# A second table of places for an attention, Fourier and feed-forward kernel

## The chip, the cores and the metric

The kernel runs on one core of a Trainium2 chip. A core has five engines that run side by side, each with its own instruction stream, worked through strictly in order: TensorE (PE) multiplies matrices, VectorE (DVE) and ScalarE (ACT) do elementwise work, GpSimd (POOL) does elementwise work and issues some transfers, and SyncE (SP) issues most transfers. The engines wait for each other on semaphores. The metric is the device time of one execution, in microseconds (us); lower is better. The kernel before took 1082.76 us, the median of 3 runs (1081.66 to 1085.46).

## The reference

There are 8 batches, each with 8 heads, 576 positions and 64 channels per head. The attention part adds two results: a full softmax attention over queries, keys and values that are averaged in groups of four positions, repeated back to full length, and a softmax attention in which a position sees only neighbours less than 4 away. The heads are laid side by side to x with 512 channels, and then:

```python
X = np.fft.fft(np.fft.fft(x, axis=1), axis=2)
u = x + np.real(X)
un = (u - mean(u)) / np.sqrt(var(u) + 1e-6)
out = u + np.maximum(un @ w_ch1, 0.0) @ w_ch2     # 512 -> 2048 -> 512
```

## The kernel before, in words

**Stages.** Of each batch, five overlapping stretches of the sequence are five units (class Unit). A unit's queries and keys come in by one transfer (`Unit.load`, line 707), its values by another (`Unit.load_v`, line 711). PE makes the local scores (line 740), DVE the maxima (752), ACT the exponentials (759), PE transposes them (772) and multiplies by the values (800), and DVE scales the result (820) into one of two tiles, xa or xb, that all batches share. Beside it class Pooled does the averaged attention of a whole batch: `sum_in` (DVE, 723) adds up queries and keys of every unit in groups of four, `pool_v` (PE, 567) does it for the values of all five units, and `scores` (593), `values` (642) and `result` (660) work on the sums in three groups.

**Fourier stage.** Class Mix folds the batch (`cross`, `channels`, `fold`), multiplies along the sequence on PE (`sequence`, 909), then along the channels (`mix`, 945 and 949), and DVE unfolds the result (968). Three kinds of rows go out to memory on SP's queue: xa and xb as they are (`store_local`, 1001 and 1002, to tensors ux), the mixed rows (`store_mixed`, 982, to tensors um) and the last rows of a pair of batches (`store_ends`, 988). xa and xb can be written for the next batch only when `store_local` has read them.

**Feed-forward.** The 36 tiles of 128 rows are taken in blocks of four. Blocks 0 to 2 (class Block) load the parts, sum them, normalise, transpose (`turn`, 1162) and multiply: `first` is twelve matmuls (1189), `high` and `low` (ACT 1193, DVE 1197) split the hidden row in two parts, `second` is twelve matmuls (1209 to 1211), `finish` (1214) adds the input. Products of two split numbers take three matmuls. The other blocks run in pairs (class Super) by a scheme with seven products in place of eight (`product`, 1348), which needs sums of the inputs (`add_up` on POOL, 1315, `sum_high` on ACT, 1326, `sum_low` on DVE, 1330) and differences of the weights. Class Differences makes those, one after another for eight pairs of weight tiles: `rejoin` (DVE, 1069) adds two parts of a weight tile into the tiles raws[0] and raws[1], `differ` (POOL, 1079) subtracts quarters of them from each other, `high` (ACT, 1083) and `low` (POOL, 1087) split the differences, and `keep` (SP, 1092) stores them.

**Chains that matter below.** The tiles raws are few. The next `rejoin` overwrites what `differ` reads, and the next `differ` overwrites what `keep` stores. The same raws serve later as scratch: raws[0] holds a transposed tile that `sum_high` and `sum_low` read, and it then takes `save` (ACT, 1368), which copies the first product out of its bank so that PE may go on adding to that bank. All PE results go to eight banks; a step that needs a bank waits until the one that used it is done.

**The order.** Every step is put into a list by the function `at`. For each kind of step the table TURNS holds a list of numbers, its places, one for each instance in the order in which the program's plans name them; the list of steps is sorted by place, and in that order each engine gets its instructions. The places run from 0 to 1954, up to the first steps of the paired blocks. Later steps have due times that a plan computes, and come after all places. No scheduler changes the order, so an instruction that waits holds up all behind it on its engine.

```python
    def at(fn, *args, t=0.0):
        ...
        place = next(places.get(name, iter(())), None)
        events.append((place is None, t if place is None else place, len(events), partial(fn, *args)))
    ...
    with tc.manual_schedule():
        for *_, fn in sorted(events, key=lambda e: e[:3]):
            fn()
```

Of the kernel before, what the change touches and what calls it, by code (L numbers as in the profile page):

```python
# [27 lines left out]
        49, 124, 252, 388, 530, 652, 781, 917,  # L28
    ),
    "Pooled.copy_v": (  # L30
        51, 131, 256, 395, 535, 659, 789, 918,
    ),
    "Pooled.scores": (
        38, 30, 33, 138, 95, 104, 270, 210, 229, 394, 347, 367, 539, 489, 505, 672, 604, 605, 786, 749, 759,
        937, 864, 890,
    ),
    "Pooled.maxima": (
        54, 32, 36, 149, 98, 110, 275, 212, 234, 402, 356, 382, 545, 495, 511, 675, 608, 614, 796, 751, 761,
        945, 873, 895,
    ),  # L40
    "Pooled.exps": (
        64, 37, 44, 154, 107, 125, 280, 215, 242, 418, 372, 393, 552, 504, 531, 688, 613, 629, 797, 757, 773,
        950, 878, 914,
    ),
    "Pooled.transpose_p": (
        83, 39, 61, 179, 117, 135, 303, 224, 274, 424, 381, 408, 555, 521, 544, 707, 623, 681, 814, 763, 793,
        953, 881, 923,
    ),
    "Pooled.copy_p": (
        85, 41, 66, 183, 122, 146, 308, 233, 279, 437, 386, 413, 569, 529, 558, 718, 634, 683, 819, 768, 811,  # L50
        955, 886, 936,
    ),
    "Pooled.values": (
        92, 53, 80, 192, 132, 153, 312, 267, 287, 439, 403, 425, 581, 540, 559, 720, 668, 694, 837, 804, 822,
        957, 925, 949,
    ),
    "Pooled.result": (
        94, 59, 86, 193, 137, 160, 317, 269, 293, 449, 409, 430, 591, 546, 570, 722, 674, 705, 843, 815, 825,
        963, 939, 951,
    ),  # L60
    "Pooled.store": (
        88, 251, 328, 522, 656, 770, 938, 968,
    ),
    "Pooled.pack": (
        112, 209, 345, 462, 601, 726, 869, 975,
    ),
    "Mix.cross": (
# [3 lines left out]
    ),  # L71
    "Mix.channels": (
# [4 lines left out]
    ),  # L77
    "Mix.fold": (
# [4 lines left out]
    ),  # L83
    "Mix.split_z": (
        99, 141, 194, 254, 349, 377, 501, 499, 577, 654, 710, 798, 852, 909, 987, 999,
    ),
    "Mix.sequence_z": (
        159, 316, 433, 513, 702, 824, 964, 1029,
    ),
    "Mix.z_high": (  # L90
        173, 335, 447, 518, 711, 829, 981, 1034,
    ),
    "Mix.z_low": (
        199, 337, 463, 528, 714, 836, 1000, 1098,
    ),
    "Mix.sequence": (
        216, 200, 175, 181, 338, 336, 332, 319, 476, 483, 458, 459, 573, 578, 600, 599, 762, 745, 742, 736,
        875, 876, 847, 854, 1001, 1007, 990, 995, 1052, 1045, 1071, 1081,
    ),
    "Mix.sequence_out": (  # L100
        228, 190, 344, 342, 488, 469, 588, 606, 764, 747, 885, 855, 1021, 1008, 1066, 1108,
    ),
    "Mix.mix": (
        257, 307, 243, 311, 401, 419, 354, 359, 366, 450, 502, 498, 516, 571, 626, 648, 609, 642, 677, 682,
        775, 808, 792, 833, 896, 919, 930, 982, 900, 988, 1060, 1085, 1030, 1047, 1117, 1147, 1179, 1203,
        1150, 1217,
    ),
    "Mix.even_out": (
        258, 244, 404, 371, 373, 507, 527, 632, 620, 695, 785, 807, 898, 946, 911, 1074, 1038, 1119, 1195,
        1156,  # L110
    ),
    "Mix.unfold": (
        333, 325, 331, 330, 423, 427, 378, 379, 466, 461, 510, 525, 602, 587, 662, 655, 644, 647, 703, 698,
        834, 839, 862, 857, 932, 935, 984, 992, 1050, 1046, 1123, 1101, 1094, 1102, 1185, 1173, 1252, 1250,
        1249, 1248,
    ),
    "Mix.store_mixed": (
        357, 436, 624, 828, 904, 1058, 1152, 1267,
    ),
    "Mix.store_local": (  # L120
        115, 184, 273, 292, 389, 380, 512, 572, 671, 667, 784, 865, 922, 961, 996, 1004,
    ),
    "Mix.store_ends": (
        562, 831, 1199, 1306,
    ),
    "Unit.load": (
        2, 4, 11, 13, 10, 25, 62, 29, 50, 47, 130, 139, 144, 143, 176, 263, 291, 187, 253, 245, 390, 302,
        412, 250, 387, 589, 481, 560, 547, 456, 661, 717, 686, 396, 687, 787, 845, 821, 791, 755,
    ),
    "Unit.sum_in": (  # L130
        3, 8, 17, 27, 14, 55, 75, 46, 58, 56, 174, 168, 188, 180, 191, 276, 339, 313, 334, 323, 472, 397,
        465, 398, 451, 594, 584, 585, 564, 586, 743, 746, 724, 679, 737, 799, 861, 846, 820, 806,
    ),
    "Unit.load_v": (
# [32 lines left out]
        48,  # L167
    ),
    "close_b": (
        993,  # L170
    ),
    "close_a": (
        1013,
    ),
    "close_e": (
        1167,
    ),
    "close_d": (
        1317,
# [1542 lines left out]
```

## Time and profile before

| what | value |
|---|---|
| runs | 1082.76 us median (1081.66 to 1085.46) |
| profiled execution, its own time | 1078.42 us |
| span of its trace | 1076.6 us |
| PE busy | 1036.2 us, 96% of the span |
| DVE, ACT, POOL busy | 640.1, 389.7 and 328.7 us |
| HBM traffic | 143.22 MB read, 56.43 MB written |

The span is the time from the first to the last instruction of the trace; the execution's own time holds 1.8 us more. Busy is the time in which an engine executes. A view by windows tells how busy each engine is in a stretch, a timeline gives the instructions in order, with the idle time before them in brackets and what ended it, and the chain of work that ended last follows the program back from its last instruction. PE's clock has two levels, 1.2 and 2.4 GHz; the granted clock is given as a share of the higher one.

### The profile page before, as it was taken

The numbers are of one execution on the slowest core, as the hardware profiler recorded it, in microseconds if no ns is written. First come the engines' busy times: TensorE is split into PE (matmuls) and PEld (weight loads), VectorE is DVE, ScalarE is ACT, GpSimd is POOL, SyncE is SP. The second block draws the span as 40 slices with busy tenths as digits, with TensorE's granted clock in tenths as the row PEclk, the third lists the DMA queues.
The fourth block names the chain that finished last, engine by engine and source line by source line (L and its number), as shares of the span: only waits on it lengthen the run. The fifth ranks groups of instructions, "written<-read, shape, count | busy, mean of one in ns | idle before, by whom it ended". The sixth has DMA issues, their size and how long they took to land.

```text
span 1076.6 us, 21807 instructions
## 1 busy us (share of the span) xinstructions
PE 1036.2 (96%) x8296; PEld 831.4 (77%) x8296; DVE 640.1 (59%) x1226; ACT 389.7 (36%) x1069; POOL 328.7 (31%) x486
## 2 busy tenths in 40 slices
PE   6899999999999999989998999999999999999998
PEld 4677767777877788878886888887788887888886
DVE  6999979889997884354354333564334465333332
ACT  6775667664443442122241111252111143111121
POOL 1222223224654556464641121253212033200000
PEclk9999999999999999999999999999999999999999
DMA  9567768865745554865836787946978643953242
GB/s 349 185 233 237 239 180 243 253 177 172 201 127 180 153 147 133 190 190 163 196 137 175 227 229 204 281 115 170 272 232 224 199 136 89 247 184 136 78 127 78
DMA packets 114400, 201.61 MB, mean 187 GB/s; under 512 B 13792, under 2 KB 30080, under 8 KB 114168
## 3 DMA queue, kind: packets, MB, share of 16 engines
q1 hardware_dynamic: 99752, 173.08, 48.4%
q0 software_dynamic: 14544, 27.15, 14.6%
q8 instruction: 65, 1.06, 0.4%
q14 instruction: 39, 0.32, 0.1%
HBM read 143.22 MB, written 56.43 MB: 185 GB/s over the span
## 4 chain that ended last, share of the span: by engine, by line
PE 71%; DVE 10%; DMA 9%; issue 4%; POOL 3%; SPq 1%; ACT 1%; DVEq 0%; ACTq 0%; POOLq 0%
PE banks L1348 20%; PE banks L1211 11%; PE banks L1209 11%; PE banks L1210 11%; PE banks L1189 9%; PE banks L909 3%; DMA qkT<-in_qk_dram 2%; DMA raw<-in_wq_dram 2%; DVE wt L478 1%; PE banks L1162 1%; PE banks L949 1%; DMA ux<-xb 1%; DMA ut<-um 1%; PE banks L800 1%; DMA um<-o 1%
## 5 line engine op out<-in xcount | busy, mean ns | idle before, releaser
L1209 PE MATMUL banks<-w2h,hh 128*128 128x512 f32 x576 | 228.5, 397 | 0.0
L1211 PE MATMUL banks<-w2h,hl 128*128 128x512 f32 x576 | 225.8, 392 | 2.0 <-DVE hl L1197 1.9
L1210 PE MATMUL banks<-w2l,hh 128*128 128x512 f32 x576 | 225.2, 391 | 0.0
L1193 ACT ACTIVATE hh<-row 128x512 fp32r<-128x512 f32 x72 | 45.6, 633 | 290.1 <-DVE row L1375 173.2
L1348 PE MATMUL banks<-w,w 128*128 128x512 f32 x576 | 144.9, 395 | 4.0 <-ACT raw L1368 4.0
L1189 PE MATMUL banks<-unT,w 128*128 128x512 f32 x576 | 138.2, 392 | 1.1 <-DVE ut L1214 1.1
L1348 PEld LDWEIGHTS banks<-w,w 128*128 128x128 f32 x576 | 109.0, 190 | 28.7 <-ACT raw L1368 4.9
L1211 PEld LDWEIGHTS banks<-w2h,hl 128*128 128x128 f32 x576 | 108.1, 188 | 27.0 <-DVE hl L1197 3.3
L1189 PEld LDWEIGHTS banks<-unT,w 128*128 128x128 f32 x576 | 107.9, 188 | 24.8 <-DVE ut L1214 1.5
L1210 PEld LDWEIGHTS banks<-w2l,hh 128*128 128x128 f32 x576 | 108.2, 188 | 22.6
L1209 PEld LDWEIGHTS banks<-w2h,hh 128*128 128x128 f32 x576 | 108.3, 188 | 22.5
L1197 DVE SCALAR_TENSOR_TENSOR hl<-row,hh 128x512 fp32r<-128x512 f32 x72 | 50.4, 700 | 114.7 <-ACT hh L1193 114.2
L1348 PE MATMUL banks<-unT,w 128*128 128x512 f32 x432 | 106.2, 390 | 2.4 <-DVE w L1375 2.4
L1348 PEld LDWEIGHTS banks<-unT,w 128*128 128x128 f32 x432 | 80.8, 188 | 20.5 <-DVE w L1375 3.7
L1375 DVE TENSOR_TENSOR w<-raw,banks 128x512 f32<-128x512 f32 x48 | 33.0, 688 | 66.2 <-PE banks L1348 64.4
L1197 DVE SCALAR_TENSOR_TENSOR hl<-banks,hh 128x512 fp32r<-128x512 f32 x48 | 32.9, 686 | 65.3 <-ACT hh L1193 62.6
L759 ACT ACTIVATE sb<-banks,mx 128x64 f32<-128x64 f32 x320 | 69.8, 329 | 3.1 <-PE banks L772 1.8
L909 PE MATMUL banks<-seq,f 128*128 128x290 f32 x256 | 67.2, 411 | 2.1 <-DVE xb L820 2.1
L1193 ACT ACTIVATE hh<-banks 128x512 fp32r<-128x512 f32 x48 | 28.5, 594 | 106.9 <-PE banks L1210 73.6
L1147 POOL TENSOR_TENSOR rstd<-rstd,mhalf 128x1 f32<-128x1 f32 x36 | 23.8, 662 | 124.6 <-DVE rstd L1146 124.6
L909 PEld LDWEIGHTS banks<-seq,f 128*128 128x128 f32 x256 | 47.1, 190 | 15.0 <-DVE xb L820 2.2
L1315 POOL TENSOR_TENSOR raw<-raw 128x256 f32<-128x256 f32 x48 | 39.5, 824 | 52.8 <-ACT raw L1268 47.5
(131 smaller groups left out, 1557.2 us busy)
## 6 DMA issues: line engine op xcount, KB each, us to landing
w<-ut SPq DMA_DIRECT2D x96, 256.0 KB
qkT<-in_qk_dram SPq DMA_DIRECT2D x40, 512.0 KB
w<-ub SPq DMA_DIRECT2D x72, 256.0 KB
raw<-in_wq_dram SPq DMA_DIRECT2D x64, 256.0 KB
uh<-w SPq DMA_DIRECT2D x42, 256.0 KB
vaug<-in_vw_dram SPq DMA_DIRECT2D x40, 260.0 KB
out_dram<-ut SPq DMA_DIRECT2D x36, 256.0 KB
um<-o SPq DMA_DIRECT2D x16, 512.0 KB
```

Of the source, the lines that this page charges most:

```text
L759: nc.scalar.activation(out=self.sb[:, hp, z], in_=self.sc[:, z, hp], func=AF.Exp, scale=0.125, bias=self.mx[:, z, hp : hp + 1],)
L909: nc.tensor.matmul(y, l, r, start=(i == 0), stop=(i == len(mms) - 1))
L1147: nc.gpsimd.tensor_tensor(out=rstd, in0=rstd, in1=mhalf, op=ALU.pow)
L1189: nc.tensor.matmul(hps, a[:, c, :], unT[:, x, c, :], start=(i == 0), stop=(i == len(mms) - 1))
L1193: nc.scalar.activation(out=hh, in_=self.hps[f], func=AF.Relu)
L1197: nc.vector.scalar_tensor_tensor(out=hl, in0=self.hps[f], scalar=0.0, in1=self.hh[f].bitcast(F32), op0=ALU.max, op1=ALU.subtract)
L1209: nc.tensor.matmul(acc, hh, w2h, start=start, stop=False)
L1210: nc.tensor.matmul(acc, hh, w2l, start=False, stop=False)
L1211: nc.tensor.matmul(acc, hl, w2h, start=False, stop=stop)
L1315: nc.gpsimd.tensor_tensor(out=out, in0=a, in1=b, op=op)
L1348: nc.tensor.matmul(self.ps[into], w[:, y, c, :], both[z][:, c, :], start=(start and i == 0), stop=(i == len(mms) - 1), skip_group_check=True)
L1375: nc.vector.tensor_add(out=out, in0=raws[a], in1=self.ps[x])
```

## The change

The numbers in TURNS are others; nothing else. Every stage's instances keep their number and their work, and the same steps are emitted in another sequence. Of the table, these lists show the kind of edit (one place for each batch or each pair of weight tiles):

```diff
     "Pooled.pool_v": (
-        49, 124, 252, 388, 530, 652, 781, 917,
+        55, 110, 251, 387, 523, 648, 778, 897,
     ...
     "Differences.rejoin": (
-        1552, 1566, 1613, 1649, 1676, 1735, 1748, 1779,
+        1552, 1575, 1636, 1663, 1700, 1740, 1751, 1784,
     "Differences.differ": (
-        1556, 1584, 1616, 1664, 1694, 1738, 1764, 1795,
+        1554, 1601, 1644, 1676, 1712, 1748, 1776, 1810,
```

The first place is SP's queue in the middle of the Fourier stage, where batch 5's rows of xb (to ux_70) and the mixed rows of batch 3 (from tiles o to um_76) are stored. Before:

```order
L707 DMA qkT<-in_qk_dram 128x1024
L982 DMA um_76<-o_3140 128x2x512
L982 DMA um_76<-o_3153 128x2x512
L988 DMA um_75<-ends 34x512
L988 DMA um_76<-ends 34x512
L988 DMA um_75<-ends 34x512
L988 DMA um_76<-ends 34x512
L707 DMA qkT<-in_qk_dram 128x1024
L1001 DMA ux_70<-xb 56x3x512
L1001 DMA ux_70<-xb 3x1x512
L1001 DMA ux_70<-xb 56x2x512
L1001 DMA ux_70<-xb 2x1x512
```

The same place in the changed kernel:

```order
L1002 DMA ux_70<-xa 4x512
L707 DMA qkT<-in_qk_dram 128x1024
L1001 DMA ux_70<-xb 56x3x512
L1001 DMA ux_70<-xb 3x1x512
L1001 DMA ux_70<-xb 56x2x512
L1001 DMA ux_70<-xb 2x1x512
L1002 DMA ux_70<-xb 3x512
L982 DMA um_76<-o_3157 128x2x512
L982 DMA um_76<-o_3235 128x2x512
L707 DMA qkT<-in_qk_dram 128x1024 x2
```

The stores of xb stood behind two stores of mixed rows and four of ends; now they stand ahead of the mixed rows, and the ends come later still.

The second place is DVE's queue at the end of block 1. The rows with raw are a `rejoin` into raws[0] and raws[1]; those with hl are `low` of a hidden row, and those with un the normalisation of a tile of block 2. Before (the fifth rejoin, of w18 and w19):

```order
L1154 TENSOR_SCALAR un_6516<-ut02_171,mv_6496,rstd_6499 128x512
L1197 SCALAR_TENSOR_TENSOR hl_6541<-banks_201,hh_6507 128x512
L1069 TENSOR_TENSOR raw_162<-w18_5153 128x512
L1069 TENSOR_TENSOR raw_4801<-w19_5506 128x512
L1154 TENSOR_SCALAR un_6568<-ut01_170,mv_6510,rstd_6513 128x512
L1197 SCALAR_TENSOR_TENSOR hl_6578<-banks_201,hh_6539 128x512
L1171 TENSOR_TENSOR unT0_4748<-banks_201,unT0_4748 128x4x128 x4
```

The same place in the changed kernel (the fourth rejoin, of w16 and w17):

```order
L1146 TENSOR_SCALAR rstd_6537<-mv_6534 128x1
L1069 TENSOR_TENSOR raw_162<-w16_4956 128x512
L1069 TENSOR_TENSOR raw_4791<-w17_4959 128x512
L1154 TENSOR_SCALAR un_6542<-ut03_172,mv_6534,rstd_6537 128x512
L1197 SCALAR_TENSOR_TENSOR hl_6545<-banks_201,hh_6513 128x512
L1171 TENSOR_TENSOR unT0_4732<-banks_201,unT0_4732 128x4x128
L1197 SCALAR_TENSOR_TENSOR hl_6577<-banks_201,hh_6528 128x512
L1171 TENSOR_TENSOR unT0_4732<-banks_201,unT0_4732 128x4x128 x3
```

The chain of differences now runs one pair of weight tiles later here. The `differ` that this rejoin waits for is at place 1644 and the rejoin at 1663; before they were at 1664 and 1676.

The third place is DVE's queue at the hand-over from block 2 to the first paired blocks, up to the first `combine` (the last row of each). The rows with w12 to w17 are `sum_low`; raw_162 is raws[0] in both. Before:

```order
L1330 TENSOR_TENSOR w13_4808<-raw_4802,w12_4805 128x2x128
L1330 TENSOR_TENSOR w13_4808<-raw_162,w12_4805 128x2x128
L1330 TENSOR_TENSOR w15_5144<-raw_4803,w14_4811 128x2x128
L1330 TENSOR_TENSOR w17_5150<-raw_4802,w16_5147 128x2x128
L1214 TENSOR_TENSOR ut00_169<-banks_201,ut00_169 128x512
L1290 TENSOR_TENSOR unT0_4748<-wt_4804,unT0_4748 128x2x128 x2
L1330 TENSOR_TENSOR w17_5150<-raw_162,w16_5147 128x2x128
L1375 TENSOR_TENSOR row0_5527<-raw_162,banks_201 128x512
```

The same place in the changed kernel:

```order
L1330 TENSOR_TENSOR w13_4798<-raw_162,w12_4795 128x2x128
L1214 TENSOR_TENSOR ut00_169<-banks_201,ut00_169 128x512
L1330 TENSOR_TENSOR w13_4798<-raw_4792,w12_4795 128x2x128
L1290 TENSOR_TENSOR unT0_4732<-wt_163,unT0_4732 128x2x128
L1290 TENSOR_TENSOR unT0_4732<-wt_4794,unT0_4732 128x2x128 x2
L1330 TENSOR_TENSOR w17_4959<-raw_4792,w16_4956 128x2x128
L1375 TENSOR_TENSOR row0_5507<-raw_162,banks_201 128x512
```

The last reader of raw_162 ahead of the combine was the last `sum_low`; now it is an earlier one, with six instructions behind it.

## Rows read from the trace of the kernel before

**Rows 1.** The profile's page, busy time by engine; the chain that ended last, by engine.
```profile
PE 1036.2 (96%) x8296; PEld 831.4 (77%) x8296; DVE 640.1 (59%) x1226; ACT 389.7 (36%) x1069; POOL 328.7 (31%) x486
...
PE 71%; DVE 10%; DMA 9%; issue 4%; POOL 3%; SPq 1%; ACT 1%; DVEq 0%; ACTq 0%; POOLq 0%
```
**Rows 2.** View by windows: us, each engine's busy time, granted clock, DMA share, GB/s.
```profile
0.00:50.00 50.00, 37.58 (x959) 28.27 (x963) 38.88 (x81) 34.68 (x129) 11.55 (x28) 1.00 0.73 260
...
150.00:250.00 100.00, 93.93 (x1906) 71.43 (x1896) 85.74 (x200) 66.58 (x232) 27.38 (x49) 0.98 0.69 206
...
450.00:575.00 125.00, 118.51 (x534) 96.50 (x534) 60.10 (x105) 35.37 (x83) 62.50 (x84) 0.99 0.62 171
575.00:1076.60 501.60, 494.39 (x2192) 405.19 (x2190) 209.05 (x348) 111.70 (x205) 90.96 (x110) 1.00 0.62 180
```
**Rows 3.** Timeline of PE: start, duration, what, [idle before it <- what ended it].
```profile
27.13 1.16 PE L800 MATMUL banks<-vaug,pT 64*64 64x65 f32 x64 [2.27 <-DVE odt L660]
...
44.82 0.51 PE L593 MATMUL banks<-sums 64*32 64x160 f32 x16 [1.37 <-DVE odt L660]
...
158.32 0.82 PE L593 MATMUL banks<-sums 64*64 64x160 f32 x16 [2.10 <-DVE xb L820]
...
224.44 1.73 PE L909 MATMUL banks<-seq,f 128*128 128x290 f32 x6 [2.05 <-DVE xb L820]
...
467.48 0.66 PE L1162 MATMUL banks<-ident,un 128*128 128x128 f32 x4 [3.09 <-DVE hl L1197]
...
569.11 4.31 PE L1348 MATMUL banks<-w,w 128*128 128x512 f32 x12 [2.60 <-ACT raw L1368]
```
**Rows 4.** Chain that ended last, 200 to 226 us: start, duration, what.
```profile
203.21 9.15 DMA um<-o
...
212.38 10.75 DMA ux<-xb
```
**Rows 5.** Chain that ended last, 143 to 160 us.
```profile
148.40 5.75 DMA qkT<-in_qk_dram
```
**Rows 6.** Timeline of DVE and POOL, 459 to 468 us, and DVE at 477 us.
```profile
460.57 1.42 POOL L1079 TENSOR_TENSOR wt<-raw 128x256 f32<-128x256 f32 x2
...
462.03 3.15 DVE L1069 TENSOR_TENSOR raw<-w 128x512 f32<-128x512 f32 x2 [2.38 <-POOL wt L1079]
...
466.74 0.68 DVE L1197 SCALAR_TENSOR_TENSOR hl<-banks,hh 128x512 fp32r<-128x512 f32 x1
...
477.80 1.38 DVE L1069 TENSOR_TENSOR raw<-w 128x512 f32<-128x512 f32 x2
```
**Rows 7.** Timeline of DVE and ACT, 565 to 570 us.
```profile
566.70 0.68 DVE L1214 TENSOR_TENSOR ut<-banks,ut 128x512 f32<-128x512 f32 x1
567.30 0.75 DVE L1290 TENSOR_TENSOR unT<-wt,unT 128x256 fp32r<-128x256 f32 x2
567.97 0.42 DVE L1330 TENSOR_TENSOR w<-raw,w 128x256 fp32r<-128x256 f32 x1
...
568.48 0.58 ACT L1368 COPY raw<-banks 128x512 f32<-128x512 f32 x1 [3.56 <-DVE w L1330]
```
**Rows 8.** Timeline of PE, 584 us.
```profile
584.05 2.92 PE L1348 MATMUL banks<-w,w 128*128 128x512 f32 x12
```
**Rows 9.** Timeline of SP and PE, 33 to 39 us.
```profile
33.98 0.78 PE L593 MATMUL banks<-sums 64*64 64x160 f32 x16
...
34.64 1.69 SPq L711 DMA_DIRECT2D vaug<-in_vw_dram  x1
...
38.78 1.69 PE L567 MATMUL banks<-vaug,poolm 128*32 128x260 f32 x20 [0.34 <-DMA vaug<-in_vw_dram]
```
**Rows 10.** Timeline of POOL and DVE, 479 to 512 us.
```profile
483.53 1.44 POOL L1079 TENSOR_TENSOR wt<-raw 128x256 f32<-128x256 f32 x2 [2.05 <-DMA ut<-wt]
...
485.84 2.23 DVE L1069 TENSOR_TENSOR raw<-w 128x512 f32<-128x512 f32 x2
...
511.35 1.55 POOL L1079 TENSOR_TENSOR raw<-raw 128x256 f32<-128x256 f32 x2 [4.93 <-DMA ut<-raw]
```

More of the change, by code (lines that the diff above doesn't have):

```diff
@@ L36 @@
+        926, 865, 889,
     ),
     "Pooled.maxima": (
-        54, 32, 36, 149, 98, 110, 275, 212, 234, 402, 356, 382, 545, 495, 511, 675, 608, 614, 796, 751, 761,
-        945, 873, 895,
+        45, 33, 40, 140, 105, 108, 288, 212, 226, 405, 358, 392, 544, 492, 525, 672, 614, 625, 811, 750, 756,
+        933, 876, 900,
     ),
     "Pooled.exps": (
-        64, 37, 44, 154, 107, 125, 280, 215, 242, 418, 372, 393, 552, 504, 531, 688, 613, 629, 797, 757, 773,
-        950, 878, 914,
+        68, 39, 57, 153, 106, 136, 292, 218, 231, 411, 371, 396, 555, 503, 530, 689, 617, 644, 816, 758, 776,
@@ L44 @@
+        936, 878, 902,
     ),
     "Pooled.transpose_p": (
-        83, 39, 61, 179, 117, 135, 303, 224, 274, 424, 381, 408, 555, 521, 544, 707, 623, 681, 814, 763, 793,
-        953, 881, 923,
+        79, 50, 66, 181, 111, 145, 295, 224, 264, 425, 378, 404, 558, 510, 548, 697, 633, 671, 820, 768, 803,
+        949, 888, 913,
     ),
     "Pooled.copy_p": (
-        85, 41, 66, 183, 122, 146, 308, 233, 279, 437, 386, 413, 569, 529, 558, 718, 634, 683, 819, 768, 811,
-        955, 886, 936,
+        83, 53, 72, 196, 117, 149, 302, 228, 274, 434, 380, 409, 566, 516, 556, 705, 640, 681, 823, 773, 814,
@@ L52 @@
+        953, 891, 934,
     ),
     "Pooled.values": (
-        92, 53, 80, 192, 132, 153, 312, 267, 287, 439, 403, 425, 581, 540, 559, 720, 668, 694, 837, 804, 822,
-        957, 925, 949,
+        84, 63, 77, 198, 137, 163, 310, 265, 293, 438, 401, 431, 576, 543, 562, 710, 659, 688, 832, 793, 819,
+        960, 921, 944,
     ),
     "Pooled.result": (
-        94, 59, 86, 193, 137, 160, 317, 269, 293, 449, 409, 430, 591, 546, 570, 722, 674, 705, 843, 815, 825,
-        963, 939, 951,
+        91, 64, 82, 202, 148, 170, 315, 271, 298, 441, 402, 433, 578, 546, 568, 716, 668, 694, 842, 809, 828,
@@ L116 @@
+        840, 830, 869, 873, 931, 930, 989, 1004, 1026, 1049, 1124, 1134, 1101, 1086, 1202, 1196, 1231, 1220,
+        1272, 1275,
     ),
     "Mix.store_mixed": (
-        357, 436, 624, 828, 904, 1058, 1152, 1267,
+        352, 452, 598, 796, 882, 1054, 1182, 1237,
     ),
     "Mix.store_local": (
-        115, 184, 273, 292, 389, 380, 512, 572, 671, 667, 784, 865, 922, 961, 996, 1004,
+        107, 156, 260, 279, 370, 403, 519, 550, 653, 684, 775, 791, 918, 905, 990, 1000,
     ),
     "Mix.store_ends": (
-        562, 831, 1199, 1306,
+        564, 898, 1153, 1280,
@@ L164 @@
-        556, 596, 610, 622, 719, 735, 748, 738, 753, 826, 850, 882, 893, 866, 948, 972, 980, 977, 986,
+        29, 87, 75, 92, 100, 141, 160, 205, 223, 229, 296, 307, 325, 348, 351, 417, 435, 482, 476, 497, 623,
+        571, 591, 615, 620, 711, 727, 744, 748, 755, 827, 846, 887, 895, 864, 958, 975, 980, 971, 984,
     ),
     "constants": (
-        48,
+        52,
     ),
     "close_b": (
-        993,
+        988,
     ),
     "close_a": (
-        1013,
+        1010,
     ),
     "close_e": (
-        1167,
+        1087,
@@ L227 @@
     "Half.load": (
-        1722, 1355, 1730, 1448, 1767, 1677, 1732, 1332, 1814, 1382, 1824, 1415, 1801, 1810, 1829, 1817, 1846,
-        1825, 1746, 1660, 1781, 1680, 1820, 1769,
+        1747, 1389, 1772, 1402, 1806, 1591, 1725, 1510, 1766, 1568, 1797, 1717, 1743, 1715, 1808, 1721, 1819,
+        1752, 1729, 1813, 1782, 1836, 1811, 1867,
     ),
     "Half.stats": (
-        1804, 1726, 1828, 1551, 1876, 1857, 1859, 1798,
+        1812, 1623, 1847, 1736, 1834, 1796, 1860, 1897,
     ),
     "Half.norm": (
-        1821, 1774, 1837, 1572, 1883, 1868, 1867, 1896,
+        1840, 1705, 1852, 1781, 1854, 1880, 1887, 1904,
@@ L236 @@
     ),
     "Half.turn": (
-        1835, 1822, 1847, 1854, 1894, 1892, 1869, 1914,
+        1844, 1839, 1861, 1807, 1888, 1881, 1902, 1907,
     ),
     "Half.turn_copy": (
-        1850, 1845, 1853, 1855, 1908, 1901, 1913, 1915,
+        1850, 1851, 1866, 1859, 1893, 1896, 1916, 1917,
     ),
     "Half.turn_high": (
-        1844, 1851, 1912, 1899,
+        1846, 1872, 1909, 1911,
     ),
     "Half.turn_low": (
-        1852, 1863, 1918, 1919,
+        1862, 1877, 1921, 1928,
     ),
     "Half.turn_keep": (
-        1860, 1886, 1911, 1921,
+        1856, 1865, 1918, 1926,
```

117 lines of the change are left out of this document (57 added, 60 removed), and 102 rows, old and new, of the table TURNS.

## The prediction

> **What bounds the kernel now.** I read the page first: PE is busy 1036.2 of 1076.6 us, and the chain that ended last is PE for 71% of its length [rows 1]. The change removes no work from any engine, so it can only act on the 40.4 us in which PE stood idle (1076.6 - 1036.2), on the time in which its clock was at the lower level, and on new waits. The view by windows says where the idle time lies: from 575 us on PE is busy 494.39 of 501.60 us [rows 2], 7.2 us of idle time in the half of the program whose order has no places and stays. That leaves 40.4 - 7.2 = 33.2 us before 575 us; 12.4 us of it are in the first 50 us, 6.1 us from 150 to 250 us, 6.5 us from 450 to 575 us [rows 2]. Then PE's own timeline, for the single waits. The six longest that I weigh are 2.27, 1.37, 2.10, 2.05, 3.09 and 2.60 us, and the bracket names what ended each [rows 3]. Last, for each of them, the chain or the other engine's timeline, to see what was really late. The first of those belongs to the start, where PE has too little data for any order to help it much; I leave it.
>
> Everything is counted against the profiled execution (1078.42 us, its span 1076.6 and 1.8 around it). The median of the runs is 4.3 us above that execution; I carry the sum over to the median, 1082.76 us.
>
> **The change, part by part.**
>
> *Stores of xb (222 us).* PE waited 2.05 us for a DVE step that writes xb [rows 3]. The chain there is the store of mixed rows, 9.15 us, and behind it the store of xb, 10.75 us, to 223.1 us [rows 4]; only then may the next batch write xb. SP's queue shows why: the stores of xb stood behind six stores of Fourier results, and now stand ahead of them. The 9.15 us no longer lie before the store of xb, over four times the wait of PE. So I take the whole wait, **-2.0 us**; bounds 0 (the same DVE step is then late for something else) and -2.05. The mixed rows leave later in return; they are read by the feed-forward blocks tens of us behind, which is their cover.
>
> *Loads of batch 5 (156 us).* PE waited 2.10 us at the averaged scores, with a load of queries and keys in the chain that landed 5.75 us after its issue [rows 3, 5]. In the table the last load of that batch stood 15 places ahead of these scores (589 and 604), now 36 (569 and 605). The clock was at 0.98 of the higher level over the 100 us around it [rows 2], which is up to 2 us of work at the lower level's pace. Bounds 0 and -4.1; I take **-2.0 us**, near the wait itself, since the sums on DVE for this batch have come nearer to the scores.
>
> *Rejoin at the end of block 1 (464 us).* DVE waited 2.38 us until POOL had done with raws, then took 3.15 us for two additions that take 1.38 us elsewhere, and reached the hl that PE waited for at 466.74 us; PE stood for 3.09 us [rows 3, 6]. Now the rejoin there is one pair of tiles behind, 19 places after the differences it waits for in place of 12, so POOL should be done in time: of the 3.09 us, the 2.38 us of waiting go. The other 0.71 us hang on the slow additions, and these I keep, since POOL has splits of differences beside the rejoin in both orders. **-2.4 us**, bounds 0 and -3.1.
>
> The slow pair, 3.15 us beside POOL's work against 1.38 us, is what the Trainium skill speaks of ("SBUF — State Buffer", section "SBUF: two separate sides"): VectorE with two SBUF inputs and a GpSimd operation share a port pair under an exclusive lock, and whoever comes second waits for the whole instruction. The trace agrees in kind. By that rule no move helps as long as POOL reads beside the additions; if the new place is free of POOL's work, the rule frees the 0.7 us as well, and the sum below would be -9.2 in place of -8.5 us.
>
> *Hand-over to the paired blocks (566 us).* PE waited 2.60 us for the copy `save` [rows 3], and that waited 3.56 us for a DVE sum that ended at 568.39 us [rows 7]. It is the write into raws[0], behind the last reader of it on DVE. In the new order that reader is earlier: behind it stand one finish (0.68), a sum (0.42), three late lows (0.75 for two, so 1.1) and a sum (0.42), together 2.6 us by [rows 7]. The copy could then start near 565.8 us, after the first products, and PE about 2.5 us earlier. The next thing that could be late is the second half of w13, which PE reads four matmuls into the next product; it stands 1.5 us before the end of the same DVE row of work, at about 566.9 us, still in time. The twelve matmuls after the wait took 4.31 us, where twelve take 2.92 us later [rows 3, 8]: 1.4 us that the lower clock cost, which goes if the gap goes. **-3.9 us**, bounds 0 and -4.0.
>
> *Averaged scores of batch 1 (43 us).* PE waited 1.37 us for a bank that an averaged result held [rows 3]. In PE's new order the third group of scores comes ahead of the averaged product that this result belongs to, so that wait has no object: **-1.4 us**, bounds 0 and -1.4.
>
> *What comes nearer to its cover.* Three places speak against the change.
> First, `pool_v` needs the values of all five units, and its first places but one have moved forward: 124 to 110 for batch 1, while the last of its loads still needs a buffer that a product of an early unit frees. Before, that load was issued at 34.64 us and PE waited 0.34 us for it at 38.78 us, so a landing takes up to 4.1 us from the start of the issue [rows 9]. Now PE has some 3.2 us of work between (a unit's scores and values, two groups of averaged scores of 0.78 us each as in [rows 9], a transposition). **+1.0 us**, bounds 0 and +2.5.
> Second, the load of unit 19 stood 56 places ahead of batch 3's averaged scores (291 and 347), now 14 (332 and 346), about as near as the load at 156 us was, which cost 2.10 us [rows 3]. **+1.2 us**, bounds 0 and +4.
> Third, in block 2 the sixth and seventh rejoin (places 1740 and 1751) now stand next to each other on DVE, and the second waits for a whole `differ` in between. That takes four subtractions and a wait for stored tiles: 1.44 us for two and 2.05 us of waiting [rows 10], so about 5 us, and then the rejoin itself 2.23 us [rows 10]. PE has four groups of twelve matmuls, some 11 us by [rows 8], before it needs the next hl, which covers this; with a wait of 4.93 us for a store, as there was one at 511 us [rows 10], it doesn't. **+1.0 us**, bounds 0 and +4.
>
> Sum: -2.0 - 2.0 - 2.4 - 3.9 - 1.4 + 1.0 + 1.2 + 1.0 = **-8.5 us**. All other moves, on some 20 us of idle time that I did not name, I take as nothing on balance; they may give or take 6 us. The profiled execution would come to 1069.9 us, the median to 1082.76 - 8.5 = **1074.3 us**.
>
> **The rivals.**
>
> *The waits only move.* Every engine has the same work, and in the attention stage DVE is nearly as full as PE (85.74 of 100 us against 93.93 from 150 to 250 us [rows 2]). A wait of PE that is removed there is given back at the next step for which DVE is late. Then of the five gains only the hand-over and the rejoin stay, -6.3 us, and about as much comes back as new waits: 1083 us, no change. For it: DVE's share. Against it: from 450 us on DVE has half its time free (60.10 of 125 us [rows 2]), so nothing there takes the two gains back.
>
> *The values come too late in every batch: slower.* The mechanism of the first nearer place, in all eight batches. If a load of values lands not 4.1 but 5.75 us after its issue, as the load of queries and keys did [rows 5], PE waits 5.75 - 3.2, some 2.5 us, at each `pool_v`: 8 x 2.5 = 20 us more. With the gains, 11.7 us, that is +8 us, 1091 us. It decides once a landing takes over 3.2 + 11.7 / 8 = 4.7 us on average. For it: the store and load rows of 5.75 to 10.75 us [rows 4, 5] show that transfers queue up. Against it: the trace before has one wait for values, 0.34 us [rows 9], and most later batches keep more work between.
>
> *All the idle time that an order can reach goes.* Of the 33.2 us before 575 us some 10 are the start. If the table has also loosened the smaller waits, most of the rest goes, 20 us with the clock: 1063 us. For it: each of the five waits that I followed has been loosened, and no other part of the table is known to me to be worse than by the three places above. Against it: PE would have to run at 99% from 50 us on.
>
> *The change does nothing to what is waited for.* The moved steps would stand where nothing hangs on them. The three places in the queues rule that out; I give it no chance of its own.
>
> **How the numbers follow.** The forecast, a gain of 4 to 14 us, 0.50; the larger gain 0.15; waits that only move, 0.17; slower by late values or the like, 0.18. About 0.3% (3.2 us) is what a measurement of this kernel can tell from no change. Faster 0.50 + 0.15 = 0.65, same 0.17, slower 0.18. The range for 8 in 10 takes in the larger gain down to 1063 us and the waits that only move, and part of the slower case: 1063 to 1088 us. The forecast's own range is 1069 to 1079 us.
>
> **What would show it.** Right: no gap of PE over 1 us at the block-2 transpositions and at the hand-over, and twelve matmuls there in 2.9 us; PE not waiting for xb before the Fourier matmuls of batch 5; PE's idle time before the hand-over near 25 us. Wrong: waits of PE for values at `pool_v` of 1 us or more in several batches; a gap before the averaged scores of batch 3; DVE standing over 6 us before a rejoin in block 2 with PE idle behind it; or a lower granted clock in a stretch where it was full.

## The result and the profile after

The changed kernel is slower: 1092.45 us (median of 10 runs, 1087.49 to 1098.09) against 1082.7 us (10 runs), a ratio of 1.0088 with a 95% interval of 1.0060 to 1.0116. That is 9.5 us by the ratio, where 8.5 us less were forecast; it lies outside the range of 1063 to 1088 us. The profiled execution took 1093.14 us, its span 1091.4 us, 14.8 us more than that of before.

The page of the changed kernel: busy time, share, instructions.

```profile
PE 1044.1 (96%) x8296; PEld 837.9 (77%) x8296; DVE 633.1 (58%) x1226; ACT 390.5 (36%) x1069; POOL 328.5 (30%) x486
```

With [rows 1]: PE is busy 7.9 us longer with the same instructions, and idle 47.3 us (1091.4 - 1044.1), 6.9 us longer. The view by windows, cut at the hand-over (columns as in [rows 2]):

```profile
0.00:50.00 50.00, 37.03 (x903) 28.39 (x905) 37.06 (x77) 33.58 (x122) 9.79 (x26) 0.97 0.75 263
150.00:250.00 100.00, 93.86 (x1841) 71.01 (x1833) 88.36 (x189) 66.33 (x231) 27.32 (x46) 0.99 0.70 210
450.00:590.00 140.00, 129.24 (x581) 105.72 (x580) 64.49 (x123) 38.11 (x88) 75.07 (x102) 0.96 0.63 167
590.00:1091.40 501.40, 493.26 (x2181) 404.29 (x2179) 208.00 (x347) 111.72 (x205) 90.70 (x110) 1.00 0.62 179
```

The two last windows (501.4 us here, 501.6 us in [rows 2]) don't begin at the same matmul. Counted from the same twelve matmuls ahead of the hand-over (562.22 us before, 577.73 us here) and behind it (577.11 and 589.47 us), the 14.8 us are 15.5 us more ahead of the hand-over, 3.1 us less in it, and 2.4 us more behind it. The part behind has no places in the table and holds the same order; its 2.4 us are one wait for a `save` in the paired blocks and the twelve matmuls behind it, in the kernel before and here:

```profile
770.22 3.02 PE L1348 MATMUL banks<-w,w 128*128 128x512 f32 x12 [1.44 <-ACT raw L1368]
783.40 4.61 PE L1348 MATMUL banks<-w,w 128*128 128x512 f32 x12 [2.29 <-ACT raw L1368]
```

The longer busy time goes with the clock: 0.96 of the higher level from 450 to 590 us, where [rows 2] has 0.99 from 450 to 575 us, and 0.97 in the first 50 us, where it has 1.00.

PE's timeline in the changed kernel, its longer waits (columns as in [rows 3]):

```profile
8.59 1.13 PE L740 MATMUL banks<-qkT 64*64 64x64 f32 x32 [4.05 <-DMA qkT<-in_qk_dram]
44.54 0.87 PE L623 MATMUL banks<-ident,sd 128*128 128x128 f32 x6 [1.25 <-DVE xa L820]
47.31 0.43 PE L733 MATMUL banks<-bits 64*64 64x256 bf16 x4 [1.46 <-DVE odt L660]
73.77 1.47 PE L567 MATMUL banks<-vaug,poolm 128*32 128x260 f32 x18 [1.75 <-DMA vaug<-in_vw_dram]
221.21 0.91 PE L800 MATMUL banks<-vaug,pT 64*64 64x65 f32 x32 [1.73 <-ACT pT L788]
246.87 0.55 PE L623 MATMUL banks<-ident,sd 128*128 128x128 f32 x3 [2.31 <-DVE odt L660]
302.51 2.08 PE L1189 MATMUL banks<-unT,w 128*128 128x512 f32 x4 [1.54 <-ACT even L956]
348.82 0.50 PE L1211 MATMUL banks<-w2h,hl 128*128 128x512 f32 x1 [2.06 <-DVE hl L1197]
469.33 4.81 PE L1189 MATMUL banks<-unT,w 128*128 128x512 f32 x12 [8.95 <-DVE hl L1197]
580.45 4.33 PE L1348 MATMUL banks<-w,w 128*128 128x512 f32 x18
586.59 1.66 PE L1348 MATMUL banks<-unT,w 128*128 128x512 f32 x6 [1.80 <-DVE w L1375]
```

Five of the six waits of [rows 3] were followed in the prediction, and none of the five is here as it was. One new wait, 8.95 us at the end of block 1, is larger than the 8.5 us that I had forecast as the whole gain, and the twelve matmuls behind it took 4.81 us where twelve take 2.88 us at the higher clock. It is followed back on POOL and DVE, first POOL:

```profile
453.97 0.56 POOL L1147 TENSOR_TENSOR rstd<-rstd,mhalf 128x1 f32<-128x1 f32 x1 [9.78 <-DVE rstd L1146]
454.50 0.87 POOL L1132 DMA_DIRECT2D ut<-ux  x1
...
460.57 1.19 POOL L1136 DMA_DIRECT2D ut<-ud  x1
```

and DVE:

```profile
465.13 0.69 DVE L1143 BATCH_NORM_STATS2 st<-ut 128x6 f32<-128x512 f32 x1 [8.70 <-DMA ut<-ud]
...
467.39 1.28 DVE L1069 TENSOR_TENSOR raw<-w 128x512 f32<-128x512 f32 x2
468.59 0.68 DVE L1197 SCALAR_TENSOR_TENSOR hl<-banks,hh 128x512 fp32r<-128x512 f32 x1
```

POOL stood 9.78 us at the small power (pow, L1147) that norms tile 0 of block 2, because DVE reached that tile's statistics late, behind a `low` that waits, through the `high` on ACT, for PE. Behind the power in POOL's queue stand the last five accumulating loads of block 2's tiles (L1132, L1136). They went out from 454.50 us on, the one that matters at 460.57 us, and DVE, which stood 8.70 us at the statistics of tile 2, could read it at 465.13 us. Behind these in DVE's queue stand the norm, the rejoin and then the `low` (468.59 us) without which PE has no free bank. In the order of before two of these five loads stood ahead of the first power of block 2 and two more ahead of the second, and POOL's longest such wait from 430 to 462 us was 3.69 us.

The other new waits of the middle look the same in the timelines of the engines that PE waited for (SP's rows are issues of stores):

```profile
217.98 0.44 ACT L462 ACTIVATE wt<-raw 128x256 f32<-128x256 f32 x1 [5.24 <-DMA raw<-in_wq_dram]
...
232.40 5.42 SPq L1001 DMA_DIRECT2D ux<-xb  x4
...
242.92 5.41 SPq L673 DMA_DIRECT2D ud<-odt  x7
...
246.39 0.42 DVE L660 TENSOR_TENSOR odt<-banks,rsd 128x256 f32<-128x256 f32 x1 [2.81 <-DMA ud<-odt]
...
298.54 0.69 DVE L1143 BATCH_NORM_STATS2 st<-ut 128x6 f32<-128x512 f32 x1 [2.29 <-DMA ut<-ud]
```

At 218 us ACT stood 5.24 us for a piece of weights, with the exponentials and the copy of pT behind it that PE waits for at 221 us; this step (`size` of piece 8) has moved from place 921 to 844. At 246 us DVE stood 2.81 us until a store had read odt; the store was issued at 242.92 us, behind the stores of both xb and xa of batch 6, of which that of xb moved ahead of it (place 961 to 905). At 298 us it is a landing again.

### The profile page after: what moved, and what is told of

The parts are those of the page before. It is cut to its first block, busy times and chain, and to the rows that moved or that the text cites. A ratio compares the mean times of both kernels' runs of the same rounds, so it can differ in the third digit from the quotient of the medians.

```text
span 1091.4 us, 21813 instructions
## 1 busy us (share of the span) xinstructions
PE 1044.1 (96%) x8296; PEld 837.9 (77%) x8296; DVE 633.1 (58%) x1226; ACT 390.5 (36%) x1069; POOL 328.5 (30%) x486
## 5 line engine op out<-in xcount | busy, mean ns | idle before, releaser
L1189 PE MATMUL banks<-unT,w 128*128 128x512 f32 x576 | 142.6, 400 | 10.6 <-DVE hl L1197 9.0
L1189 PEld LDWEIGHTS banks<-unT,w 128*128 128x128 f32 x576 | 110.7, 193 | 35.9 <-DVE hl L1197 9.4
L1348 PE MATMUL banks<-unT,w 128*128 128x512 f32 x432 | 106.2, 390 | 3.4 <-DVE w L1375 3.4
L1348 PEld LDWEIGHTS banks<-unT,w 128*128 128x128 f32 x432 | 80.9, 188 | 21.5 <-DVE w L1375 4.7
L909 PE MATMUL banks<-seq,f 128*128 128x290 f32 x256 | 67.3, 412 | 0.5 <-ACT yf L916 0.5
L1147 POOL TENSOR_TENSOR rstd<-rstd,mhalf 128x1 f32<-128x1 f32 x36 | 23.6, 656 | 133.9 <-DVE rstd L1146 133.9
L909 PEld LDWEIGHTS banks<-seq,f 128*128 128x128 f32 x256 | 47.2, 190 | 14.0 <-issue 1.4
```

Source lines behind the costliest of these rows:

```text
L909: nc.tensor.matmul(y, l, r, start=(i == 0), stop=(i == len(mms) - 1))
L1147: nc.gpsimd.tensor_tensor(out=rstd, in0=rstd, in1=mhalf, op=ALU.pow)
L1189: nc.tensor.matmul(hps, a[:, c, :], unT[:, x, c, :], start=(i == 0), stop=(i == len(mms) - 1))
L1348: nc.tensor.matmul(self.ps[into], w[:, y, c, :], both[z][:, c, :], start=(start and i == 0), stop=(i == len(mms) - 1), skip_group_check=True)
```

## Experiments

In each, only places in the table are set; a splice takes one kernel's order up to a place and the other's for the rest. The diffs are sketches of the order on the engines named, shortened at `...`; load(2,1,1), for one, is part 1 of tile 1 of block 2, and high(1,12) piece 12 of block 1. Ratios are to the kernel before on the same chip (medians 1082.0 to 1084.5 us); us are worked out from them with 1083 us.

**The stall at 469 us.** Theory: POOL's loads behind the power. Rival: the rejoin, or the order on DVE.

```diff
 differ(1)
+load(2,1,1) load(2,2,2) load(2,3,1) load(2,1,2) load(2,3,2)
 stats(2,0)                      # the power on POOL
-load(2,1,1) ... load(2,1,2) ... load(2,2,2) ... load(2,3,1) ... load(2,3,2)
```

> The changed kernel with one thing moved: the last five accumulating loads of block 2's tiles stand on POOL ahead of the first pow that waits for DVE, instead of behind it. Theory A (the 8.95 us stall of PE at 469 us is these loads, held behind POOL's wait): the stall goes, with about 2 us of work at the lower clock behind it, so 9 to 11 us less than the changed kernel: 1081 to 1084 us, and no wait of PE over 3 us between 450 and 480 us. Rival B (the rejoin itself, or the banks, are late whatever the loads do): the stall stays over 5 us, 1088 us or more. Rival C (the loss is the lower clock all over the kernel): less than 4 us gained, 1089 us or more.

Measured: 1085.25 us, ratio 1.0025 (1.0003 to 1.0046), 7.2 us under the changed kernel by the medians; the two profiled executions are 10.9 us apart (spans 1091.4 and 1080.5). POOL in this run:

```profile
442.23 0.85 POOL L1132 DMA_DIRECT2D ut<-ux  x1
...
450.38 0.88 POOL L1136 DMA_DIRECT2D ut<-ud  x1 [2.50 <-DMA ut<-ux]
452.13 0.57 POOL L1147 TENSOR_TENSOR rstd<-rstd,mhalf 128x1 f32<-128x1 f32 x1 [0.87 <-DVE rstd L1146]
```

The loads go out while POOL would have stood. The window from 450 to 500 us shows what it does to PE, in this run

```profile
450.00:500.00 50.00, 49.62 (x224) 40.25 (x223) 25.83 (x50) 12.49 (x28) 29.05 (x42) 1.00 0.60 182
```

and in the changed kernel:

```profile
450.00:500.00 50.00, 41.05 (x179) 33.25 (x178) 22.20 (x41) 9.80 (x21) 25.74 (x35) 0.90 0.49 127
```

Idle time and the lower clock (0.90) go together. PE's longest wait from 450 to 480 us is 0.38 us; the rivals would have left the stall. The median is 1 us above what I expected.

The other half of the test left the loads and moved what PE needed ahead of the statistics on DVE:

```diff
 high(1,12)
+high(1,13)
 norm(2,0)
+low(1,12) low(1,13)
 stats(2,2)
 ...
-low(1,12) high(1,13) ... low(1,13)
```

> The changed kernel with the two `low` rows that PE needed at 469 us (pieces 12 and 13 of block 1, and `high` of piece 13) ahead of the statistics on DVE that stood 8.70 us for a landing; the five loads stay where the change put them, behind POOL's wait. Theory A (the root is POOL's queue: the loads go out late whatever DVE does first): PE gets one product and two rounds of work earlier and then stands again, at the `low` of piece 14, behind the next statistics; 3 us less than the changed kernel, 1088 to 1091 us, with a wait of over 5 us between 460 and 480 us. Rival (the order on DVE alone is the fault): the stall goes as in r1_loads, 1083 to 1086 us.

Measured: 1093.09 us, ratio 1.0109 (1.0064 to 1.0154, 6 runs): no gain seen, where 3 us were expected, though the two intervals together leave room for them. The rival's 1083 to 1086 us are out. PE's waits there:

```profile
461.38 0.65 PE L1162 MATMUL banks<-ident,un 128*128 128x128 f32 x4 [1.86 <-DVE un L1154]
...
471.86 1.12 PE L1162 MATMUL banks<-ident,un 128*128 128x128 f32 x4 [5.47 <-DVE hl L1197]
```

Two waits, 7.3 us together, at the next tiles in place of one. As long as the loads go out late, DVE's order only chooses which step is late.

**Where the rest of the loss lies.** Three repairs of the same kind on top of r1_loads (the new places only):

```diff
 ACT   z_high(5), exps(33), copy_p(34), sequence_out(5,1)
+      size(8)
 SP    ends of batches 2 and 3
+      store(6) of averaged results
       store_local(6,1)          # xb
 DVE   low(0,2), join(17)
+      stats(1,0)
```

> The run r1_loads with three more repairs of one kind, each for a step that waits for a transfer ahead of something that PE needs: on ACT the step `size` of piece 8, which stood 5.24 us for its weights at 218 us, goes behind the Fourier copies of batch 5; on SP the stores of the averaged results of batch 6 go ahead of the stores of xb of batch 6, behind which DVE stood 2.81 us at 246 us; the statistics of block 1's tile 0, for which DVE stood 2.29 us at 298 us, go behind `low` of piece 2. Theory A (each of these standings is what PE waited for: 1.7, 2.3 and 0.9 to 2.4 us): 5 to 7 us under r1_loads (1085.25 us), that is 1078 to 1080 us, under the kernel before. Rival (the waits only move to the next late step): within 2 us of r1_loads, 1083 to 1087 us.

Measured: 1079.73 us, ratio 0.9967 (0.9947 to 0.9987), 6.3 us under r1_loads by the ratios. The waits at 221 and 247 us are gone (their two moves were made together, so no run parts them); from 150 to 250 us PE is busy 97.55 us instead of 93.86. The third repair failed: PE's wait there grew.

```profile
298.07 2.50 PE L1189 MATMUL banks<-unT,w 128*128 128x512 f32 x5 [4.68 <-POOL w L496]
```

DVE now stood 2.13 us for the landing of the next tile, and POOL's power for that tile stood ahead of the split steps. So this tile's statistics go back too, and a `high` and a `low` ahead of two `size` steps that wait for weights:

```diff
 DVE   norm(1,0)
+      stats(1,1)
       join(20), join(18), norm(1,1)
 ACT   size(32)
+      high(1,3)
       size(33), size(34)        # DVE: low(1,3) ahead of join(34)
```

> The run r3_queues with two more steps of the same kind put behind: the statistics of block 1's tile 1, for whose landing DVE stood 2.13 us while the pow and then the split steps on POOL and ACT waited, and PE 4.68 us, at 298 us; and `high` and `low` of piece 3 of block 1 ahead of two `size` steps on ACT that stood 3.43 us for weights at 338 us (PE: 2.12 us). Theory A (one kind of fault, each price adds): 5 to 7 us under r3_queues (1079.73), 1073 to 1075 us. Rival (the waits move on): 1078 to 1081 us.

Measured: 1077.19 us, ratio 0.9915 (0.9883 to 0.9948), 5.6 us (1.5 to 9.8) under r3_queues by the ratios. The absolute time is above the expectation; 0.9915 of the 1083.07 us of r3_queues' chip is 1073.9 us, inside it (this chip ran the kernel before in 1084.47 us). PE's windows:

```profile
150.00:250.00 100.00, 97.76 (x1942) 73.98 (x1932) 92.64 (x202) 69.25 (x244) 28.20 (x49) 1.00 0.72 210
450.00:575.00 125.00, 122.22 (x548) 99.67 (x547) 60.38 (x114) 37.47 (x87) 67.99 (x93) 0.99 0.65 176
```

So the changed order with eleven of its 1955 steps moved is 9.2 us faster than the kernel before (5.6 to 12.7 us by the interval). It and s4r_late_part, below, beat both kernels and can't be told apart from each other.

**The two terms at the end.** The order of before up to place 1410, the changed order with the mended loads behind it:

> The order of before up to place 1410 (about 362 us) and the changed order behind it, with the five loads of r1_loads in their repaired place. It carries only the two gains that the prediction counted as largest, the rejoin at the end of block 1 (-2.4 us) and the hand-over (-3.9 us). Theory A (both are real once the loads are in time): 3 to 6 us under before, 1076 to 1079 us against 1082.3, with no wait of PE over 1 us at the end of block 1 and under 2 us at the hand-over. Rival (the hand-over's wait has another cause, and only the rejoin's 3.1 us goes): 1079 to 1080 us with a wait at L1348 of 1.5 us or more. Rival 2 (given back): 1082 us.

Measured: 1076.03 us, ratio 0.9937 (0.9914 to 0.9960), 6.8 us faster. No wait of PE over 0.4 us is left at the end of block 1. And with only block 2 and the hand-over from the changed order (from place 1700 on):

> The order of before up to place 1700 (about 471 us, the end of block 1), the changed order behind it: of the changed steps only block 2 and the hand-over. Beside s4r_late_part (ratio 0.9937 to before), which has the changed end of block 1 as well, it parts the two large terms. Theory A (the prediction: hand-over -3.9 us, rejoin -2.4): a ratio of 0.9964 to before, 4 us faster. Rival (of the hand-over only the second wait of 0.8 us and the first's 0.8 went, as the traces show 2.60 us shrunk to 1.80; the rejoin with its lower clock is worth the other 5 us): 1 to 2 us faster, a ratio of 0.998 to 0.999, with a wait of over 3 us at the transpositions of block 2.

Measured: 1081.03 us, ratio 0.9984 (0.9958 to 1.0009): 1.7 us faster, not told apart from no change. The old wait at the end of block 1 is still there, as expected:

```profile
466.32 0.66 PE L1162 MATMUL banks<-ident,un 128*128 128x128 f32 x4 [3.08 <-DVE hl L1197]
```

The two runs together put about 5 us on the end of block 1 (0.9937 / 0.9984; 1.4 to 8.8 us with both intervals) and about 2 us on the hand-over (-1.0 to 4.5 us). The traces measure the hand-over closer. PE there before, beside the wait of [rows 3]:

```profile
562.22 2.88 PE L1348 MATMUL banks<-unT,w 128*128 128x512 f32 x12
...
574.22 1.67 PE L1348 MATMUL banks<-unT,w 128*128 128x512 f32 x6 [0.80 <-DVE w L1375]
...
577.11 2.88 PE L1348 MATMUL banks<-unT,w 128*128 128x512 f32 x12
```

and in s4r_late_part:

```profile
562.21 2.88 PE L1348 MATMUL banks<-unT,w 128*128 128x512 f32 x12
564.92 4.33 PE L1348 MATMUL banks<-w,w 128*128 128x512 f32 x18
571.07 1.67 PE L1348 MATMUL banks<-unT,w 128*128 128x512 f32 x6 [1.80 <-DVE w L1375]
...
573.96 2.88 PE L1348 MATMUL banks<-unT,w 128*128 128x512 f32 x12
```

The first wait (2.60 us in [rows 3]) is gone and eighteen matmuls take the time that twelve took; but the wait behind it, 0.80 us before, is 1.80 us now. From the first row to the last PE takes 14.89 us before and 11.75 us here, 3.1 us less; h1_handover (11.71 us) and the changed kernel (11.74 us) agree.

**The stores of xb, alone.** The kernel before with one move:

```diff
+store_local(5,1)                # xb of batch 5
 store_mixed(3), store_ends(3), load(36)
-store_local(5,1)
```

> The kernel before with one move: the stores of xb of batch 5 stand on SP ahead of the stores of mixed rows of batch 3. Theory A (the prediction's first term): the wait of 2.05 us for xb at 224 us goes and the time falls by 2 us, to 1080.3 us against 1082.3. Rival (the wait goes, but PE comes to wait for the next late step before 260 us): no such wait in the trace, and no difference in time, 1081.5 to 1083 us.

Measured: 1085.72 us, ratio 1.0021 (1.0004 to 1.0039), 2.3 us slower (0.4 to 4.2). The wait for xb is gone, and this came instead (SP, DVE, PE; the profiled execution, 1093.13 us, was the slowest of the 12, so the sizes may be high):

```profile
216.65 0.37 SPq L707 DMA_DIRECT2D qkT<-in_qk_dram  x1
...
228.37 1.22 DVE L723 TENSOR_REDUCE sums<-qkT 128x256 f32<-128x1024 f32 x1 [5.07 <-DMA qkT<-in_qk_dram]
...
229.73 1.34 PE L593 MATMUL banks<-sums 64*64 64x160 f32 x16 [4.56 <-DVE sums L723]
```

The load of queries and keys that was issued at 208 us before stands behind all eleven stores now. Putting it ahead of them, on top of s4r_late_part (`load(36)`, then `store_local(5,1)`, then the rest):

> The run s4r_late_part (the order of before up to place 1410, the repaired changed order behind) with the stores of xb of batch 5 moved ahead of the stores of mixed rows, as in t1_store_xb, but with the load of queries and keys that stood behind these stores moved ahead of them too. Theory A (t1_store_xb lost because this load went out 8 us later; with it in time the first term of the prediction, -2 us, is there): 1074 us against 1076.0 of s4r_late_part, no wait for xb at 224 us and none over 1.5 us for sums at 230 us. Rival (the transfers of this stretch are late in any order): 1076 us or more, with a new wait before 260 us.

Measured: 1081.95 us, ratio 0.9974 (0.9949 to 0.9999), worse than s4r_late_part by 4 us. Now the mixed rows are late:

```profile
219.10 0.70 DVE L968 TENSOR_TENSOR o<-even,banks 128x512 f32<-128x512 f32 x1 [3.02 <-DMA um<-o]
...
220.33 0.69 PE L800 MATMUL banks<-vaug,pT 64*64 64x65 f32 x32 [2.31 <-DVE yz L931]
```

DVE stood 3.02 us until the store of the mixed rows had read o, and yz, which PE waited for, stands behind that step. SP's queue shows why these stores were late:

```profile
205.69 5.79 SPq L707 DMA_DIRECT2D qkT<-in_qk_dram  x2
211.57 2.52 SPq L1001 DMA_DIRECT2D ux<-xb  x4
...
214.60 1.15 SPq L982 DMA_DIRECT2D um<-o  x2
```

Between its two loads SP stood 5.0 us until PE's local scores had freed the buffer of the second one, the load that was moved, and all stores stood behind it; those of the mixed rows went out at 214.60 us, at 204.65 us in s4r_late_part. So this load was moved too far ahead. The run shows another wait of the same kind, on SP; what the first term is worth with everything else in time, no run shows.

**The loads of batch 5, alone.** In the kernel before, `load(25)` from place 589 to 569, ahead of the stores of xb of batch 3:

> The kernel before with one move: the last load of queries and keys of batch 5 stands 20 places earlier, ahead of the stores of xb of batch 3. Theory A (the prediction's second term): the wait of 2.10 us at the averaged scores at 158 us goes and the time falls by 2 us, to 1080.3 us. Rival (the wait is the point at which PE, ahead until there, meets the pace of the transfers: the run s1_start came 4 us late to it and did not wait at the scores, and ended at the time of before): the wait turns up again at one of the next steps, and the time stays within 1 us of before, 1081.5 to 1083 us.

Measured: 1080.91 us, ratio 0.9989 (0.9969 to 1.0010). Not told apart from no change; the wait shrank from 2.10 to 1.27 us and did not go.

```profile
161.12 0.77 PE L593 MATMUL banks<-sums 64*64 64x160 f32 x16 [1.27 <-DVE xb L820]
```

The traces show what became of it. Counted from the same local scores of PE (147.30 us here, 143.48 us before), the load went out 4.2 us earlier (at 148.00 us, at 148.40 us before), but DVE could read it only 1.0 us earlier (at 156.97 us, at 154.17 us before): it took 9.0 us to land, where 5.75 us were enough in [rows 5], with the stores of xb issued right behind it.

**Splices of the first 383 us.** They were to say how the loss is shared out.

> The changed kernel's order up to place 575 (about 148 us), the order of before behind it. By the two traces PE has by then done the same work 4.0 to 4.5 us later in the changed kernel. Theory A (each stretch brings its own loss, and they add up): 4 us over the kernel before, 1087 us. Rival (the first 148 us are given back where PE next waits, so only later stretches count): within 1 us of before, 1083 us.

> The changed kernel's order up to place 775 (about 200 us), the order of before behind it. Against the run with 575 places it adds the stretch of batch 5's loads, where the traces show 4.5 us of lag turn into 1.2 us of lead. Theory A (the removed wait for batch 5's loads is a real gain of about 5 us): 1 us under the kernel before, 1081.5 us. Rival (it is the lag of the stretch before, caught up, since the loads are ready by then anyway): the same as the run with 575 places or better than before by nothing; 1083 to 1087 us with no difference between the two runs.

> The changed kernel's order up to place 1450 (about 383 us), the order of before behind it, so with the old rejoin at the end of block 1 and the old hand-over. The traces show a lag of 7.1 us here. Theory A (the stretch from 200 to 383 us brings a loss of 8 us of its own, in waits for probabilities at 221 us, a transposition at 247 us and the feed-forward steps at 302 and 349 us): 1090 us. Rival (these are given back in the feed-forward blocks, and the whole difference is the stall at 469 us): 1083 us.

Measured: 1082.08 us (0.9974 to 1.0014), 1087.95 us (1.0029 to 1.0077), 1099.08 us (1.0133 to 1.0184). The first speaks for the rival; the other two came out slower than either of their expectations. The windows of the first:

```profile
0.00:150.00 150.00, 133.19 (x2749) 101.36 (x2750) 129.50 (x279) 103.13 (x369) 35.74 (x73) 0.99 0.73 239
150.00:200.00 50.00, 47.00 (x886) 35.59 (x884) 44.45 (x94) 31.05 (x108) 12.17 (x22) 1.00 0.77 226
```

In the first 150 us PE is busy 1.5 us less than before (134.71 us), and 45 matmuls behind. From 150 to 200 us it is busy 1.0 us more (45.98 before), with the wait of 2.10 us at 158 us missing and 1.11 us in its place,

```profile
156.79 4.18 PE L909 MATMUL banks<-seq,f 128*128 128x290 f32 x16 [1.11 <-DVE rest L660]
```

and by 450 us both have been busy for 423.2 us. Most of what the start loses is given back around that wait: at the Fourier matmuls (L909) of 145 us PE is 4.2 us behind the kernel before (149.19 and 145.03 us), at those of 187 us it is 1.1 us behind (187.69 and 186.60 us). Of the 4.2 us, 1.5 us are the longer wait for the very first load (4.05 and 2.53 us).

The other two can't be read as sums: at the seam, where one order's steps follow the other's, PE waits for things that neither order makes late by itself: 4.44 us at 217 us in the second run, and 9.91 us at 408 us in the third. They don't share out the loss; they only suggest that a piece of an order isn't worth the same behind another piece.

## Why the prediction was wrong, point by point

**The step that failed: the rejoin at the end of block 1, and what I took for nothing.** For the rejoin I asked whether POOL would be done with the differences in time (19 places in place of 12). It was, and the two additions took 1.28 us instead of the 3.15 us of [rows 6] (I had kept 0.71 us for slow ones). But the `low` that PE waits for hangs on everything that stands ahead of it in DVE's queue, and I didn't list that: the statistics of a tile whose loads had gone behind a waiting step on POOL. The term was -2.4 us; it came out as the 8.95 us stall, and two of my signs for "wrong" showed, DVE standing over 6 us with PE idle behind it and a lower clock in a stretch where it was full. With the loads mended (s4r_late_part against h1_handover) it is worth about -5 us by the ratios (-1.4 to -8.8). The traces show 2.7 us of wait (3.08 to 0.37 us) and, from 450 to 500 us, a granted clock of 0.97 in h1_handover and 1.00 in s4r_late_part; in the kernel before that window ran at 1.00 with the same wait, so the clock's part differs between executions. The place was right, the sign was decided by moves beside it.

**"All other moves ... nothing on balance", plus or minus 6 us.** The five loads aside, they cost about 12 us: r3_queues and r4_queues2 gave 6.3 and 5.6 us back with six moves of one kind. Where nearly all of 1955 places change, a sum over the waits that go, with all the unnamed moves at zero, leaves out the side on which the cost lies. With these places mended the order gains 9.2 us, near my 8.5; that is luck in part, as the rejoin and the hand-over alone gave 6.8 us of it (s4r_late_part) and the two terms of 2.0 us don't show in the time.

**Stores of xb, -2.0 us.** The wait went and the time did not. I bounded the term at 0 and -2.05, and named the mixed rows' cover as the feed-forward blocks that read them. I left out what else stands behind the moved stores: a load of queries and keys (t1_store_xb, 5.07 us on DVE), and the buffer o, which DVE writes again much sooner (b1_both, 3.02 us). Alone the move costs 2.3 us. In the changed kernel the like move for batch 6 stands ahead of the store of odt that PE's wait of 2.31 us at 247 us hangs on.

**Loads of batch 5, -2.0 us.** The wait is gone from the changed kernel, but s1_start shows that PE simply came later; alone the earlier place is worth 1.2 us, with an interval that holds zero. There the load went out 4.2 us earlier and landed 1.0 us earlier. At 158 us PE had caught up with its loads, and a wait there is not 2 us of the whole.

**Hand-over, -3.9 us.** The sum on DVE came earlier as worked out (in s4r_late_part the copy starts at 565.46 us, where I had 565.8), and in the changed kernel the copy waited 0.61 us instead of 3.56,

```profile
580.98 0.59 ACT L1368 COPY raw<-banks 128x512 f32<-128x512 f32 x1 [0.61 <-DVE w L1330]
```

and PE's 2.60 us and the slow matmuls went. But 6 us later the next row of DVE is late by 1.80 us instead of 0.80: 3.1 us were left on PE's path, the same in three traces (1.7 us, -1.0 to 4.5, by the times of h1_handover). The mechanism was right, the size 0.8 us too large. I had looked for the next late thing at the second half of w13 and not beyond.

**Averaged scores of batch 1, -1.4 us.** That wait is gone; 1.25 us at a transposition and 1.46 us at the next local scores, for DVE steps on xa and odt, took its place.

**What comes nearer to its cover.** Values: no wait at batch 1, but 1.75 us at batch 2, inside the bounds; nothing over 1 us at the rest, so the rival of late values, which gave the nearest time (1091 us), had the wrong cause. The load of unit 19 and the sixth and seventh rejoin left no wait of PE over 1 us.

**The rule on the shared port** (the Trainium skill, "SBUF — State Buffer", section "SBUF: two separate sides": VectorE with two SBUF inputs and a GpSimd operation that reads SBUF wait for each other). The additions ran from 467.39 to 468.67 us; beside them POOL only issued a load, at 468.23 us, and they took 1.28 us. The trace agrees, and the 0.7 us were no part of what went wrong.

## What to carry to other kernels

When an order changes, go through each in-order queue and list the steps that wait for a transfer (a landing, or a store that must have read its buffer) and what the bounding engine needs from behind them: those are the prices, not the waits that disappear. A queue that also issues transfers counts twice, as a wait on it delays every landing behind it (POOL's 9.78 us here), and a load put too far ahead waits for its buffer with all stores behind it (SP's 5.0 us in b1_both). A removed wait is worth its length only when the next late step on that path has been found and priced too.

## What the runs showed of the hardware

POOL's accumulating loads took long and uneven times from issue to landing, for the same 256 KB: by the view of transfers 3.6 to 6.1 us for the five loads of the stall (4.5 us for the one at 460.57 us), and from 232 to 248 us of the changed kernel it has one of 8.3 us.

Executions of one and the same order differ by up to 1% (the changed kernel 1087.5 to 1098.1 us, r1_loads 1080.2 to 1091.5). Two places where profiles differ without a difference of order: PE's first wait, for the first load, is 2.53 us in the kernel before and 4.79 us in t1_store_xb, with the same order up to 200 us; and the wait for `save` near 770 us is 1.15 to 2.68 us in the 14 profiles, all with the same order there, and the twelve matmuls behind it take 3.0 us in eight of them and 4.6 us in six. So two single profiles don't tell a change of 4 us in this kernel. What else sets this spread, and what moves these two waits, isn't settled.
